# Loading x of tile 1 ahead of Wk and x of tiles 2 to 7 ahead of Wv, with the steps up to the second feed-forward unit in another order and partly on other engines

## The chip, the cores and the metric

The kernel runs on one core of a Trainium2 chip. A core has five engines, each with its own queue of instructions that it works off in order: TensorE (PE in the profile; its weight loads stand apart as PEld), VectorE (DVE), ScalarE (ACT), GpSimd (POOL) and SyncE (SP), which in this kernel issues nearly all DMA transfers. The metric is the device time of one execution in microseconds (us).

## What is computed

A pre-norm transformer block on 2048 rows of width 640: linear attention with 32 heads of width 20, whose feature map is a softmax of a projection and of its negative, and a feed-forward part of width 1728 with SiLU. Inputs and output are bfloat16.

```python
def _A_ref(x, wqkv, w_phi, wo):
    qkv = (x @ wqkv) split into q, k, v and 32 heads
    pq = jnp.einsum("bhsd,hdf->bhsf", q, w_phi)
    pk = jnp.einsum("bhsd,hdf->bhsf", k, w_phi)
    phi_q = jnp.concatenate([_softmax(pq, axis=-1), _softmax(-pq, axis=-1)], axis=-1)
    phi_k = jnp.concatenate([_softmax(pk, axis=-1), _softmax(-pk, axis=-1)], axis=-1)
    kv = jnp.einsum("bhsf,bhsd->bhfd", phi_k, v)
    z  = jnp.einsum("bhsf->bhf", phi_k)
    num = jnp.einsum("bhqf,bhfd->bhqd", phi_q, kv)
    den = jnp.einsum("bhqf,bhf->bhq", phi_q, z)[..., None] + 1e-6
    return heads joined (num / den) @ wo

def _B_ref(x, w1, w2):
    return jnp.einsum("bsf,fd->bsd", _silu(jnp.einsum("bsd,df->bsf", x, w1)), w2)

h  = x + _A_ref(_layernorm(x), A_wqkv, A_w_phi, A_wo)
h2 = h + _B_ref(_layernorm(h), B_w1, B_w2)
```

(The line that splits qkv and the one that joins the heads are shortened to words.)

## The kernel before

The 2048 rows are 16 tiles of 128 rows, t = 0 to 15. Row p * 16 + t of x stands in partition p of tile t, so that one load brings some tiles for all partitions.

The order of all work is written out by hand. ORDER (line 18) is a list of 791 step names; a loop at the end (line 903) calls the step of each name, and a step issues one or a few instructions on its engine. Each engine and each queue then runs its own instructions in the order of the list; waits for data and for free buffers follow from what the steps read and write. A dictionary ON (line 142) says on which engine a step runs where there is a choice, and WARM (line 134) is the number of warm-up matmuls.

The steps, with the lines that issue them (t is a tile, c one of five 128-row chunks of the width, g a half of the output columns):

- X0, X1, X2, X4, X8 (line 161): loads of x, of tiles 0, 1, 2 to 3, 4 to 7 and 8 to 15, 160 KB a tile, on SP's queue. WKc and WVc (line 164): loads of the key and value columns of wqkv, chunk by chunk, 160 KB each. wph0, wph1 (lines 346, 348): the feature weights w_phi in a second layout. load0 to load11 (line 488): wo, w1 and w2 for later.
- warmN (line 215): a 256-column matmul of constants whose result nobody reads.
- The key fold. Projection and feature weights are multiplied ahead, so that one matmul of x gives the keys' features. wkc (line 290) transposes chunk c of Wk on TensorE, wkec (line 307) copies the result out of PSUM, fkc (line 314) multiplies it with phi, which phi_a and phi_b (line 277) build on VectorE, and fkce (line 323) copies that into Wfk.
- The query fold: wqr (line 386) loads a transposed block of wqkv by DMA, phq (line 367) builds phi_q on GpSimd from what own (line 352) made, fqr (line 398) multiplies, fqre (line 404) copies into Wfq.
- Layer norm of tile t: stt (line 432) the moments on VectorE, rst the inverse standard deviation, on GpSimd (lines 441 and 444) or as Ln and Exp on ScalarE (lines 438 and 439), xnt (line 448) the normalized rows on VectorE or GpSimd, xtt the transpose into XnT: for tiles 0 to 3 on TensorE (line 455) with a copy xt on ScalarE or VectorE (line 475, steps x0 to x3), from tile 4 by DMA on SP's queue (line 477).
- Keys and values of tile t: Kt and Vt (line 496) ten 320-column matmuls each; those of tile 0 go chunk by chunk (K0.c line 523, V0.c line 508). ext (line 551) two Exp on ScalarE, sut (line 555) sums on VectorE, rkt (line 563) the inverse of the sums on ScalarE, sct (line 568) a scaling on VectorE, vet (line 572) a copy of the values on ScalarE, kvt (line 587) eleven small matmuls that add the tile to the key-value matrix, in PSUM banks 6 and 7, over all tiles. onesi (line 227) fills constant columns of the buffers of keys and values, mask (lines 245, 239), zeros, eqp and pad other constants, all on GpSimd. bd0, bd1 (line 596) turn the finished key-value matrix into a block-diagonal one.
- Queries: Qt (line 534), qet (line 656), qst (line 660), qrt (line 668 on), qtt (line 684, a transpose by DMA).
- Attention: Dt (line 709), Etg (lines 721, 722: division), ott (line 733: transpose by DMA), Gtg (line 742: output projection), gatg (line 749: residual).
- Second layer norm: lst, lrt, hnt, htt (the last a transpose by DMA, line 769).
- Feed-forward, in units of 2, 4, 4, 4 and 2 tiles that are named by their first tile: uN.f (line 824) and uN.L (line 835), SiLU in sN.f (line 844), ltN (line 856), dtg (line 864), oatg (line 873), outt (line 878).

PSUM has eight banks. Up to the step halves, ps_pair (line 114) hands out banks 0 to 5 as three pairs in turn to wk, xt, fk, fq, K, V and Q steps; a step that takes a pair waits until the reader of what was in it three turns earlier is done. After halves all eight banks go round one by one.

The DMA transfers complete on semaphores that are used in turn, so an issue on SP's queue can also wait for the landing of an earlier transfer.

Of the kernel before, what the change touches and what calls it, by code (L numbers as in the profile page):

```python
# [43 lines left out]
d51 ht8 lr9 hn9 oa21 ga101 G110 out2 ga100 ga110 oa50 oa40 G111 qs14 d41 oa51 D12 ls10 ht7 E120 ht9 u6.1
u6.0 oa41 ga111 u6.12 u6.8 D13 s6.0 s6.1 qr14 s6.8 E121 s6.12 u6.11 ot12 u6.2 u6.3 qr15 lr10 s6.11 u6.L
s6.2 E130 ls11 out4 E131 u6.9 qt15 s6.3 G120 ot13 s6.L u6.6 lt6 s6.6 lr11 u6.7 u6.10 hn10 u6.5 out5 s6.7
hn11 s6.9 u6.4 qt14 G121 ga120 ga121 s6.5 ht11 G130 D14 G131 E140 ga131 s6.10 s6.4 d60 ls12 oa60 d61 d70
ht10 lr12 E141 d91 ga130 ls13 oa61 hn12 oa70 D15 lr13 d90 ht12 ot14 d71 hn13 ht13 out6 G140 oa71 oa90
u10.L oa91 ga140 out9 E150 u10.0 u10.1 out7 E151 u10.6 G141 u10.9 s10.L s10.0 s10.6 u10.8 ga141 d80
u10.7 s10.1 u10.3 u10.11 ot15 s10.3 u10.5 u10.12 oa80 s10.9 s10.8 s10.11 u10.2 u10.4 ls14 s10.7 s10.5  # L50
u10.10 s10.12 s10.4 G150 G151 lt10 lr14 d81 s10.10 s10.2 d110 hn14 oa81 ht14 out8 d111 ga150 d120 ga151
ls15 d101 lr15 d100 hn15 oa100 oa110 ht15 oa101 d121 oa111 out10 oa120 out11 u14.L u14.4 u14.0 oa121
s14.0 s14.L u14.8 u14.6 s14.6 u14.2 d131 u14.12 u14.10 s14.2 s14.4 d130 lt14 oa130 oa131 s14.12 s14.10
# [887 lines left out]
```

## Time and profile before

| | us |
|---|---|
| median of 3 runs (lowest, highest) | 237.5 (237.11, 237.62) |
| the profiled execution | 237.18 |
| its span, first to last instruction | 235.1 |
| TensorE busy | 230.1 |
| VectorE busy | 166.5 |
| ScalarE busy | 104.9 |
| GpSimd busy | 59.9 |
| wk2 / wk3 start | 3.98 / 5.49 |
| K0 starts / its last matmul block ends | 10.34 / 11.70 |
| kv9 starts / kv15 starts / u2.2 starts | 56.83 / 68.59 / 112.56 |

The page gives for each engine the busy time, and in its second part the span in 40 slices of 5.9 us with the busy share in tenths:

```profile
## 2 busy tenths in 40 slices
PE   8999999998999999999999999999999999999995
PEld 5777767776777777877545777645677455778874
DVE  3899998999999999998999896792471330404031
ACT  3998997896869774620234100054300326001410
POOL 5699999990000012211010111011020010100000
```

TensorE is busy from end to end. VectorE is full until about 115 us and then half idle; GpSimd is full from about 10 to 50 us, while it normalizes; ScalarE is fullest in the first 20 us. In the timeline a row has the start, the length, the engine, the line, what is written and read, the number of instructions merged, and in brackets the idle time of the engine before it with what ended it.

Durations of the steps that the change moves: a normalization takes 2.515 us on GpSimd and 0.44 on VectorE (up to 1.00 beside one on GpSimd); the inverse standard deviation 0.80 on GpSimd and 0.50 on ScalarE; a 128x640 copy from PSUM 0.45 on VectorE and 0.70 on ScalarE; Ln and Exp of rk 0.57; the two Exp of one tile's keys 1.30; the sums of a tile's keys 1.43 to 1.48, their scaling 0.82.

### The profile page before, as it was taken

Reading aid. Unit: us, or ns where it says so; the run is one execution under the profiler, and the core shown is the slowest. Engines: PE = TensorE matmul, PEld = TensorE weight load, DVE = VectorE, ACT = ScalarE, POOL = GpSimd, SP = SyncE. Lnnn points to the kernel's source line nnn. Section 1 sums busy time; section 2 is a strip of 40 time slices with the busy share of each in tenths; the row PEclk is TensorE's granted clock in tenths of the full one; section 3 lists DMA queues with packets and bytes.
Section 4 is the critical chain, followed back from the end, with each engine's and each line's share of the span. In section 5 each row is a group of like instructions: output and inputs, shape, how many; then the busy total and the mean of one; then the engine's idle time right before and its main releaser. Section 6 shows DMA issues by size and latency. Waiting matters only on the chain.

```text
span 235.1 us, 5026 instructions
## 1 busy us (share of the span) xinstructions
PE 230.1 (98%) x1984; PEld 160.4 (68%) x1984; DVE 166.5 (71%) x351; ACT 104.9 (45%) x218; POOL 59.9 (25%) x105
## 2 busy tenths in 40 slices
PE   8999999998999999999999999999999999999995
PEld 5777767776777777877545777645677455778874
DVE  3899998999999999998999896792471330404031
ACT  3998997896869774620234100054300326001410
POOL 5699999990000012211010111011020010100000
...
GB/s 175 338 243 91 117 115 170 157 256 246 188 105 74 141 146 93 175 120 91 85 61 128 170 96 173 31 56 172 77 20 91 98 0 28 30 28 56 8 56 56
DMA packets 67213, 26.79 MB, mean 114 GB/s; under 512 B 60151, under 2 KB 66167, under 8 KB 67063
## 3 DMA queue, kind: packets, MB, share of 16 engines
...
q10 hardware_dynamic: 656, 0.03, 0.2%
q14 instruction: 7, 0.06, 0.1%
...
## 4 chain that ended last, share of the span: by engine, by line
PE 72%; DVE 17%; POOL 4%; DMA 2%; issue 2%; SPq 1%; DVEq 0%; POOLq 0%
PE banks L824 22%; PE banks L864 21%; PE banks L742 9%; PE banks L534 8%; PE banks L496 5%; DVE Sk L555 4%; DVE Sq L660 3%; POOL xn L448 3%; DVE st L432 3%; DVE EK L568 2%; PE banks L709 2%; DMA Wv<-in_A_wqkv_dram 2%; PE banks L867 2%; PE banks L587 1%; DVE xn L448 1%
## 5 line engine op out<-in xcount | busy, mean ns | idle before, releaser
L844 ACT ACTIVATE shT<-banks 128x512 bf16<-128x512 f32 (+1 forms) x53 | 28.9, 592 | 83.3 <-PE banks L824 83.3
L864 PE MATMUL banks<-w_sb,shT 128*128 128x320 bf16 (+2 forms) x429 | 61.3, 295 | 0.0
L824 PE MATMUL banks<-HnT,w_sb 128*128 128x512 bf16 (+1 forms) x325 | 59.4, 336 | 0.1
L864 PEld LDWEIGHTS <-shT 128*128 128x128 bf16 x429 | 41.2, 98 | 15.3
L824 PEld LDWEIGHTS <-w_sb 128*128 128x128 bf16 x325 | 31.2, 98 | 22.4 <-issue 0.3
L441 POOL TENSOR_SCALAR rs<-mv 128x1 f32<-128x1 f32 x28 | 8.2, 292 | 141.5 <-DVE mv L433 108.2
L873 DVE TENSOR_TENSOR o_t<-banks,X 128x320 bf16<-128x320 f32 (+2 forms) x33 | 14.8, 474 | 39.6 <-PE banks L867 26.7
L496 PEld LDWEIGHTS <-XnT 128*128 128x128 bf16 x300 | 28.4, 98 | 10.9 <-DMA XnT<-xn 0.3
L432 DVE BATCH_NORM_STATS2 st<-X 128x6 f32<-128x320 bf16 x64 | 27.8, 477 | 3.8 <-DMA X<-in_A_x_dram 3.7
L448 POOL TENSOR_SCALAR xn<-X,mv,rs 128x640 bf16<-128x640 bf16 x10 | 25.1, 2515 | 0.5
L742 PE MATMUL banks<-wo_sb,OT 128*128 128x320 bf16 x160 | 25.1, 299 | 0.0
L656 ACT ACTIVATE EQ<-banks 128x360 bf16<-128x360 f32 (+2 forms) x52 | 22.1, 514 | 5.3 <-PE banks L534 5.1
L660 DVE TENSOR_REDUCE Sq<-EQ 128x66 f32<-128x1320 bf16 x16 | 23.9, 1512 | 0.0
L749 DVE TENSOR_TENSOR X<-banks,X 128x320 bf16<-128x320 f32 x32 | 14.8, 481 | 12.8 <-PE banks L742 12.5
L534 PE MATMUL banks<-Wfq,XnT 128*128 128x360 bf16 (+2 forms) x160 | 23.3, 299 | 0.0
L555 DVE TENSOR_REDUCE Sk<-EK 128x64 f32<-128x1280 bf16 x16 | 23.0, 1460 | 0.0
L551 ACT ACTIVATE EK<-banks 128x640 bf16<-128x640 f32 x32 | 20.8, 707 | 3.7 <-PE banks L587 2.0
L496 PE MATMUL banks<-Wfk,XnT 128*128 128x320 bf16 x150 | 22.5, 299 | 0.0
L496 PE MATMUL banks<-Wv,XnT 128*128 128x320 bf16 x150 | 22.2, 299 | 0.1
L742 PEld LDWEIGHTS <-OT 128*128 128x128 bf16 x160 | 15.1, 98 | 6.3
L534 PEld LDWEIGHTS <-XnT 128*128 128x128 bf16 x160 | 15.1, 97 | 6.1
L444 POOL TENSOR_TENSOR rs<-rs,nhalf_t 128x1 f32<-128x1 f32 x28 | 16.8, 599 | 2.3
...
## 6 DMA issues: line engine op xcount, KB each, us to landing
...
```

Source lines behind the costliest of these rows:

```text
L432: nc.vector.bn_stats(st[:, i, :], X[:, t, i * HD : (i + 1) * HD])
L448: eng.tensor_scalar(out=xn_[t][:], in0=X[:, t, :], scalar1=mv_.pop(t)[:, 0:1], scalar2=rs_.pop(t)[:], op0=ALU.subtract, op1=ALU.mult,)
L496: nc.tensor.matmul(ps[:, g, 0:HD], XnT[:, c, t * P : (t + 1) * P], W[:, c, g * HD : (g + 1) * HD], start=(c == 0), stop=(c == C - 1),)
L534: nc.tensor.matmul(ps[:, 0 : e - a], XnT[:, c, t * P : (t + 1) * P], Wfq[:, c, a:e], start=(c == 0), stop=(c == C - 1),)
L551: nc.scalar.activation(E5[:, :, :, b, :], p4, AF.Exp, scale=sign)
L555: nc.vector.tensor_reduce(sk[t][:], ek[t][:, 0 : H * HF].rearrange("p (q f) -> p q f", f=DH), axis=AX.X, op=ALU.add)
L656: nc.scalar.activation(features(t, a, b)[:, :, :, i], p4, AF.Exp, scale=sign)
L660: nc.vector.tensor_reduce(sq[t][:], EQ[0][:, t, :, 0:FCH].rearrange("p c (q f) -> p c q f", f=DH), axis=AX.X, op=ALU.add)
L742: nc.tensor.matmul(ps[:, 0:HD], ot[t][:, c, :], wo_sb[:, c, g * HD : (g + 1) * HD], start=(c == 0), stop=(c == C - 1),)
L824: nc.tensor.matmul(ps[:, at : at + n], w1_sb[:, c, fc * P : fc * P + P], HnT[u][:, c, 0:n], start=(c == 0), stop=(c == C - 1),)
L844: nc.scalar.activation(shT[u][:, f0 * n : f1 * n], ps_of.pop(("u", u, f0))[:, 0 : (f1 - f0) * n], AF.Silu)
L864: nc.tensor.matmul(ps[:, 0 : b - a], shT[u][:, at : at + P], w2_sb[:, fc, a:b], start=(fc == 0), stop=False,)
```

## The change

Three things change, all in the tables at the head; no function is altered.

1. On SP's queue the load X1 goes from behind WK0 to the place behind X0, ahead of all Wk; X2 and X4 both stand ahead of the Wv loads, where X4 stood between WV0 and WV3 before; wq3 goes ahead of X8, and load6 is the first of the later loads.
2. The steps up to u2.2 stand in another order on all engines. Among others the values of tile 0 come behind the keys of tile 0, V1 ahead of V2, mask and ones at other places, and K, V, Q, D and G steps are interleaved otherwise. From ga61 and u2.2 on the order is as before. Two warm-up matmuls are dropped (20 to 18): 15 ahead of wk2 as before, three behind it instead of five.
3. Some steps run on another engine. xn1, xn2, xn5, xn6 and xn11 go from VectorE to GpSimd, xn3 and xn4 from GpSimd to VectorE; rs3, rs4, rs7, rs8, rs11 and rs12 from GpSimd to ScalarE, rs9, rs13 and rs15 the other way; wke2, x0 and fk3e from ScalarE to VectorE, wke4 from VectorE to ScalarE.

In the diff the lines of ORDER behind u2.2, which are the same words broken into lines otherwise, are left out.

```diff
 ORDER = """
-warm0 warm1 warm2 warm3 warm4 warm5 warm6 warm7 warm8 warm9 warm10 warm11 warm12 warm13 warm14 X0 WK2
-ones0 wk2 warm15 warm16 warm17 warm18 warm19 WK3 wke2 WK0 X1 WK1 st0 wk3 phi_a wke3 wk0 phi_b rs0 xn0
-wke0 own st1 xt0 wk1 fk3 WK4 wke1 X2 wk4 rs1 WV0 wke4 x0 fk1 X4 fk3e WV3 xn1 st2 st3 rs2 WV2 WV4 rs3 fk0
-fk1e fk0e fk4 WV1 V0.0 xn3 xn2 wph1 fk4e fk2 fk2e st6 xt1 wq2 K0s K0.0 K0.4 K0.3 K0.2 K0.1 ones1 x1 st4
-rs4 xt2 K1 ex0 V0.2 st5 x2 ex1 V0.3 rs6 su0 wph0 X8 rs5 K2 xn4 su1 xt4 ex2 wq3 xt3 rk0 sc0 phq V0.1
-ones6 x3 rk1 xn5 ones4 st7 ones5 V0.4 V2 su2 ve2 xt5 ve0 V1 ve1 V3 wq1 xn6 ve3 kv0 sc1 fq2 fq2e st10 K3
-st13 ones2 wq0 V4 ones3 ex3 K4 fq3 rk2 xt6 rs7 ve4 rs13 xn7 V5 ex4 xt7 st8 wq5 su3 fq3e K5 ve5 fq0 st9
-rs10 rk3 wq4 rs8 xn8 kv1 K6 sc2 rs9 kv2 sc3 ex5 xn9 st12 xt8 fq0e ex6 su4 st11 fq1 kv3 xn10 K7 fq1e ex7
-rs11 V6 rk4 su5 fq4 xn13 ve6 xt9 zeros rk5 V8 fq4e V7 sc4 ve8 ve7 xn11 kv4 fq5 st15 V9 rs12 xn12 mask
-load9 fq5e rs15 ve9 K8 xt10 su6 rk6 st14 sc5 su7 K9 kv5 ex8 rk7 su8 Q0 sc6 K10 sc7 xt13 ex9 ones7 kv6
-su9 xn15 rk8 qe0 rs14 ex10 Q1 xn14 kv7 xt11 sc8 load10 xt12 load2 xt15 qe1 K11 su10 load1 load0 V10 V13
-mask0 qs0 kv8 ex11 rk10 ve10 xt14 ve13 rk9 su11 qs1 qr1 V11 K12 sc10 ve11 rk11 K13 sc9 kv9 K14 ex12 kv10
-V12 sc11 ex13 load11 qr0 su12 ex14 load5 kv11 V14 K15 su13 su14 load4 rk12 ve12 rk13 ve14 sc12 sc13 Q2
-rk14 sc14 ex15 kv12 V15 qe2 su15 qs2 mask1 rk15 kv13 kv14 ve15 sc15 Q3 eqp qr2 qe3 kv15 Q5 qe5 Q7 bd1
-load3 halves bd0 qt0 qs3 qr3 qt1 D0 D1 E00 qe7 load6 Q4 Q9 E01 E10 E11 Q6 qe4 Q8 load7 Q10 qe9 qt2 qe6
-ot0 pad0 D2 qs4 qe8 qs5 qr4 G00 E20 ga00 G01 qe10 ot1 Q11 qr5 qt3 E21 D3 G10 ga01 E30 qt4 ls0 G11 E31
-qe11 ga10 lr0 ga11 qt5 Q14 Q12 ot2 Q13 hn0 qe14 ls1 D4 Q15 qs6 lr1 qe12 G20 qe13 qe15 ot3 G21 hn1 E40
-E41 ga20 D5 G30 G31 ga21 ht0 pad1 ht1 u0.L E50 u0.0 ot4 E51 s0.0 ga31 qr6 ga30 ls2 ls3 lr2 u0.4 u0.8 G40
-ga40 s0.8 s0.L load8 qs7 qt6 s0.4 lr3 u0.12 u0.2 hn2 ot5 G41 s0.2 qr7 u0.6 D6 ga41 ls4 u0.10 E60 hn3 lt0
-s0.6 G50 s0.12 G51 s0.10 ga51 ga50 E61 ls5 ht2 lr4 d10 d00 qt7 lr5 ht3 d01 ot6 hn4 hn5 G60 D7 qs8 G61
-qr8 d11 ht5 oa00 ht4 oa10 E70 ga61 u2.2 u2.0 ga60 qt8 E71 ot7 s2.0 oa01 qs9 u2.L qs13 s2.2 qr9 oa11 qs11
...
+warm0 warm1 warm2 warm3 warm4 warm5 warm6 warm7 warm8 warm9 warm10 warm11 warm12 warm13 warm14 X0 ones1
+X1 WK2 wk2 warm15 warm16 warm17 st0 WK3 st1 rs0 wk3 WK0 phi_b WK1 xn0 ones3 wk0 ones7 wk1 xt0 phi_a WK4
+wke2 wke1 wk4 wke3 x0 fk3 wke0 fk1 ones6 wke4 fk3e fk0 fk1e fk0e X2 X4 st2 WV0 WV1 ones5 fk4 fk2 rs1 K0s
+st3 K0.0 WV2 st4 fk4e xn1 fk2e WV3 rs2 K0.1 xt1 K0.3 st5 K0.4 K0.2 V0.0 x1 rs3 WV4 K1 V0.1 ones0 wq2 ex0
+rs4 xn3 ex1 V0.2 xn2 xt2 wph0 x2 wph1 su0 st6 wq3 V1 st7 xn4 V0.3 ve1 su1 rk0 own X8 xt3 x3 K2 ex2 su2
+rs5 phq V0.4 rs6 sc0 V2 st11 ve2 V3 xt4 xn5 st9 rs7 rk1 fq2 K3 st8 ve3 ve0 wq4 V4 fq2e ex3 xn6 rk2 xt5
+ones2 sc1 kv0 K4 ve4 V5 rs8 ex4 fq3 sc2 xn7 su3 st10 rs9 wq0 kv1 ve5 ones4 xt6 su4 K5 fq0 fq3e K6 rk3
+ex5 xt7 kv2 wq1 wq5 fq1 fq0e sc3 ex6 K7 load6 su5 fq1e mask kv3 ex7 xn8 st13 V6 xt8 mask0 rk4 ve6 rk5
+su6 sc4 rs11 fq4 fq4e xn9 zeros st12 V7 ve7 rk6 V8 rs10 sc5 xt9 xn10 load3 V9 su7 ve8 fq5 rs12 rs13 st14
+ve9 xt10 kv4 fq5e rk7 load7 K8 ex8 sc6 kv5 st15 xn11 K9 su8 xn12 sc7 Q0 kv6 K10 xt11 kv7 ex9 Q1 rk8 rs15
+load2 su9 xn13 qe0 ex10 qe1 K11 xt13 sc8 rs14 mask1 rk9 qs0 kv8 xt12 xn14 load11 V10 V13 qr0 ex11 su10
+sc9 xn15 V11 su11 kv9 xt14 rk10 ve13 ve10 K12 load4 ve11 qs1 K13 qr1 xt15 eqp K14 ex12 rk11 sc10 su12
+kv10 ex13 ex14 rk12 V12 load5 V14 sc11 su13 ve12 K15 su14 pad0 sc12 rk13 kv11 qt0 Q2 sc13 ve14 qt1 load0
+rk14 ex15 qe2 kv12 sc14 load1 su15 V15 kv13 rk15 ve15 Q3 qs2 kv14 load9 sc15 kv15 qr2 Q5 Q7 bd1 bd0 qe3
+qe5 halves D0 qs3 Q4 qt2 E00 E01 qe7 qe4 qr3 D1 Q6 E10 Q9 E11 Q8 qe6 qe9 qs4 qr4 qs5 Q10 ot0 qr5 qt3 Q11
+ot1 qe8 qe10 D2 qe11 E20 G00 G01 ga00 E21 D3 E30 qt4 E31 ga01 G10 ga10 ot2 G11 ga11 Q14 Q12 qe14 ot3 ls0
+D4 lr0 G20 Q13 ls1 G30 qe12 lr1 hn0 qt5 E40 G21 G31 hn1 E41 ht0 ht1 ga30 ga20 qs6 Q15 qe13 pad1 ga21 D5
+ga31 qs7 qr6 u0.0 E50 u0.6 qe15 E51 ls3 qr7 ls2 s0.0 load8 u0.L s0.L s0.6 u0.10 ot4 u0.12 u0.8 lr3 G40
+G41 lr2 s0.12 s0.10 u0.4 load10 hn3 qt6 ga41 ot5 ga40 u0.2 s0.8 ls4 D6 lt0 G50 qt7 E60 lr4 G51 E61 ht3
+ga51 s0.2 s0.4 d10 D7 ga50 hn4 ls5 ot6 lr5 hn2 qs8 d00 E70 hn5 oa00 ht2 d01 G60 ht4 G61 qr8 oa10 d11 ht5
+ga61 u2.2 u2.0 ga60 qt8 E71 ot7 s2.0 oa01 qs9 u2.L qs13 s2.2 qr9 oa11 qs11 u2.6 D8 u2.10 E80 ls6 qt9
...
-    WARM = 20
+    WARM = 18
...
 ON = dict(
-        wke2="ACT", wke3="ACT", rs0="POOL", xn0="DVE", wke0="ACT", wke1="DVE", rs1="POOL", wke4="DVE",
-        x0="ACT", fk3e="ACT", xn1="DVE", rs2="POOL", rs3="POOL", fk1e="ACT", fk0e="ACT", xn3="POOL",
-        xn2="DVE", fk4e="ACT", fk2e="ACT", x1="ACT", rs4="POOL", x2="ACT", rs6="ACT", rs5="POOL",
-        xn4="POOL", x3="ACT", xn5="DVE", xn6="DVE", fq2e="ACT", rs7="POOL", rs13="ACT", xn7="POOL",
-        fq3e="ACT", rs10="POOL", rs8="POOL", xn8="POOL", rs9="ACT", xn9="POOL", fq0e="ACT", xn10="POOL",
-        fq1e="ACT", rs11="POOL", xn13="POOL", fq4e="ACT", xn11="DVE", rs12="POOL", xn12="POOL", fq5e="ACT",
-        rs15="ACT", xn15="POOL", rs14="POOL", xn14="POOL",
+        rs0="POOL", xn0="DVE", wke2="DVE", wke1="DVE", wke3="ACT", x0="DVE", wke0="ACT", wke4="ACT",
+        fk3e="DVE", fk1e="ACT", fk0e="ACT", rs1="POOL", fk4e="ACT", xn1="POOL", fk2e="ACT", rs2="POOL",
+        x1="ACT", rs3="ACT", rs4="ACT", xn3="DVE", xn2="POOL", x2="ACT", xn4="DVE", x3="ACT", rs5="POOL",
+        rs6="ACT", xn5="POOL", rs7="ACT", fq2e="ACT", xn6="POOL", rs8="ACT", xn7="POOL", rs9="POOL",
+        fq3e="ACT", fq0e="ACT", fq1e="ACT", xn8="POOL", rs11="ACT", fq4e="ACT", xn9="POOL", rs10="POOL",
+        xn10="POOL", rs12="ACT", rs13="POOL", fq5e="ACT", xn11="POOL", xn12="POOL", rs15="POOL",
+        xn13="POOL", rs14="POOL", xn14="POOL", xn15="POOL",
 )
```

More of the change, by code (lines that the diff above doesn't have):

```diff
@@ L44 @@
[L44 to L53, printed above, removed]
@@ new lines @@
+ga51 s0.2 s0.4 d10 D7 ga50 hn4 ls5 ot6 lr5 hn2 qs8 d00 E70 hn5 oa00 ht2 d01 G60 ht4 G61 qr8 oa10 d11 ht5
+ga61 u2.2 u2.0 ga60 qt8 E71 ot7 s2.0 oa01 qs9 u2.L qs13 s2.2 qr9 oa11 qs11 u2.6 D8 u2.10 E80 ls6 qt9
+u2.7 u2.3 s2.L u2.11 s2.10 s2.6 qr13 E81 u2.9 s2.9 qr11 u2.5 qs12 s2.7 qs10 s2.3 u2.1 D9 G70 s2.5 E90
+qr10 u2.12 s2.11 E91 ot8 G71 u2.4 lr6 ga71 ga70 qt11 out0 lt2 s2.1 qt10 u2.8 out1 hn6 s2.4 qr12 ls7 G80
+s2.8 ga80 ot9 G81 D11 s2.12 E110 d30 ht6 qt13 E111 d20 D10 ga81 lr7 G90 E100 oa30 oa20 E101 ot10 G91 hn7
@@ new lines @@
+ga91 d31 ot11 ga90 ls8 qs15 lr8 d21 qt12 oa31 d50 G100 ls9 G101 hn8 out3 d40 d51 ht8 lr9 hn9 oa21 ga101
+G110 out2 ga100 ga110 oa50 oa40 G111 qs14 d41 oa51 D12 ls10 ht7 E120 ht9 u6.1 u6.0 oa41 ga111 u6.12 u6.8
+D13 s6.0 s6.1 qr14 s6.8 E121 s6.12 u6.11 ot12 u6.2 u6.3 qr15 lr10 s6.11 u6.L s6.2 E130 ls11 out4 E131
+u6.9 qt15 s6.3 G120 ot13 s6.L u6.6 lt6 s6.6 lr11 u6.7 u6.10 hn10 u6.5 out5 s6.7 hn11 s6.9 u6.4 qt14 G121
+ga120 ga121 s6.5 ht11 G130 D14 G131 E140 ga131 s6.10 s6.4 d60 ls12 oa60 d61 d70 ht10 lr12 E141 d91 ga130
```

12 lines of the change are left out of this document (7 added, 5 removed).

## The prediction

> **What bounds the kernel now.** First the page's head and engine table, then the chain of waits, then the list of waits on TensorE, then TensorE's timeline up to 70 us.
>
> ```profile
> span 235.1 us, 5026 instructions
> PE 230.1 (98%) x1984; PEld 160.4 (68%) x1984; DVE 166.5 (71%) x351; ACT 104.9 (45%) x218; POOL 59.9 (25%) x105
> ...
> PE 72%; DVE 17%; POOL 4%; DMA 2%; issue 2%; SPq 1%; DVEq 0%; POOLq 0%
> ...
> PE banks L587 <- DVE EK L568: 0.9, 1, 0.9
> PE banks L215 <- PEq L925: 0.8, 1, 0.8
> PE banks L398 <- DMA WTq<-in_A_wqkv_dram: 0.3, 1, 0.3
> ```
>
> TensorE is busy 98% of the span, and the change removes no matmul but two warm-ups. So it can win only what TensorE waits, and lose only new waits. The listed waits are 0.9 + 0.3 us after the start, but a matmul counts as busy to its modelled end, which hides waits shorter than the drain. The starts show them:
>
> ```profile
> 0.83 3.36 PE L215 MATMUL banks<-const-bfloat16-1.0 128*128 128x256 bf16 x15 [0.83 <-PEq L925]
> 3.98 0.74 PE L290 MATMUL banks<-ident,Wk 128*128 128x128 bf16 x5
> 4.51 1.11 PE L215 MATMUL banks<-const-bfloat16-1.0 128*128 128x256 bf16 x5
> 5.49 0.87 PE L290 MATMUL banks<-ident,Wk 128*128 128x128 bf16 x10
> ...
> 25.08 1.52 PE L496 MATMUL banks<-Wv,XnT 128*128 128x320 bf16 x10
> 26.54 1.52 PE L496 MATMUL banks<-Wfk,XnT 128*128 128x320 bf16 x10
> 28.08 0.44 PE L398 MATMUL banks<-phi_q,WTq 128*128 128x120 bf16 x5
> ...
> 32.44 1.52 PE L496 MATMUL banks<-Wv,XnT 128*128 128x320 bf16 x10
> 34.28 0.44 PE L398 MATMUL banks<-phi_q,WTq 128*128 128x120 bf16 x5 [0.32 <-DMA WTq<-in_A_wqkv_dram]
> 34.86 2.89 PE L496 MATMUL banks<-Wv,XnT 128*128 128x320 bf16 x20
> ...
> 53.09 2.88 PE L496 MATMUL banks<-Wfk,XnT 128*128 128x320 bf16 x20
> 56.83 0.51 PE L587 MATMUL banks<-VP,EK 128*128 128x63 bf16 x11 [0.86 <-DVE EK L568]
> ```
>
> A block of ten 320-column matmuls that is followed at once takes 1.36 us (20.74 to 22.10), five 120-column ones 0.27. So TensorE stands 26.44 to 26.54, 27.90 to 28.08, 33.80 to 34.28, 34.55 to 34.86 and 55.81 to 56.83: 0.10 + 0.18 + 0.48 + 0.31 + 1.02 = 2.1 us. Before kv15 (68.59) the same reading gives 0.2, and from there to the step u2.2 (112.56), where the two orders join again, nothing over 0.05. **2.3 us** is thus all there is to gain behind the opening.
>
> The second engine is VectorE. From 37 to 68.5 us it has no idle time, and kv15 on TensorE starts 0.06 us after sc15 ends (67.71 + 0.82 = 68.53). A gain must come out of VectorE as well.
>
> **The change, part by part.**
>
> **Opening, up to K0.** X1 goes ahead of the five Wk loads, so WK2, which opens the real work, is third on the queue instead of second. Landings before, in order of issue: X0 3.20, WK2 3.88, WK3 5.44, WK0 5.86, X1 6.23, WK1 6.64, WK4 7.28. All five x and Wk loads of 160 KB are equal in size. If a landing goes by its place, wk2 starts at 5.45 instead of 3.98, wk3 at 5.9 instead of 5.49, wk0 at 6.3; from WK1 on both queues have carried the same bytes, so wk1 (6.7) and wk4 (7.3) come as before. If the long step 3.88 to 5.44 belongs to Wk3 itself, WK2 lands near 4.3. I take the places; the other end is no dearer. Dropping two warm-ups (0.21 each at the slow rate) buys nothing, they ran inside this wait.
> The folds: wk4 at 7.3 to 7.7, then wke4 on ScalarE (0.7) to 8.55. VectorE now does st0, st1 (1.1 each), phi_b, xn0, phi_a, wke2, wke1, x0 (0.45 to 0.6 each) to 8.3 and fk3e (bounded by the 0.45 of a bf16 copy and twice the 0.48 of a 320-column fp32 read from PSUM; I take 0.8, nearest the latter) to 9.1. fk4 waits for fk3e's bank pair: 9.1; fk2 9.5 to 9.9. ScalarE then runs fk1e, fk0e, fk4e, fk2e at 0.65 each from 8.6 to 11.2, so K0 ends at 11.75 (before: 11.70). x1 (ScalarE, 0.65) frees K1 at 12.05. By 13.4 TensorE has K1 done, as before at 13.33, but not yet xt2 (0.27): **0.35 us behind**; I take 0.4.
>
> **Wv behind X4.** X4 (640 KB) took 2.6 us of the queue (9.18 to 11.80). Landings become X4 11.0, WV0 11.4, the last Wv near 13.5. V0.0 now comes after K0, near 11.75, V0.1 at 13.4, V1 at 14.3: hidden by 0.3 us or more. Each issue on SP's queue waits for the landing of the one eight before it (X8 was issued at 11.82, X4 landed at 11.80), so X8 now waits for WV1 (11.8) behind wq3 (1.27): 12.9 instead of 11.8, landing near 20.3 instead of 19.5. st11 on VectorE, the first reader, is due at 21.4: hidden by 1 us; if not, VectorE's queue stands.
>
> **Normalization: VectorE to GpSimd.** xn costs 2.515 us on GpSimd (x10, 25.1) and 0.44 on VectorE, up to 1.00 beside a GpSimd xn (36.56). xn1, 2, 5, 6, 11 leave VectorE, xn3 and xn4 go to it: GpSimd has 13 instead of 10 (+7.5 us), and loses rs3, 4, 7, 8, 11, 12 (0.8 each, to ScalarE at 0.5) against rs9, 13, 15: -2.4. Laying the new GpSimd order end to end: xn1 done at 10.0, xn2 13.8, xn5 20.3, xn6 22.8, xn7 25.8, xn8 29.8, xn9 33.0, xn10 36.5, xn11 39.9, xn12 42.4, xn13 45.7, xn14 49.7, xn15 52.3. Adding the 2.5 us from issue to landing of an XnT transpose, the users on TensorE come later: K7 30.7 (28.4 ready), V8 35.7 (34.5, with load6 of 480 KB ahead on the queue), V9 37.0 (35.5), K15 near 60 (55). xt2 starts at 14.0, just when xn2 is there. So hidden, the thinnest cover being 1.2 us at V8.
>
> **VectorE.** From st2 on it loses xn2 .44, xn5 .76, xn6 .35, xn11 .92 and gains xn3, xn4 (0.37 to 1.0 each, I take 0.6): -1.3. It loses the idle 0.50 (X4 landing, 11.83) and 0.78 (rs11, 36.56): -1.3. It starts st2 at 9.1 instead of 8.8: +0.3. New idle: su0 waits for ex0 0.3, sc4 and su8 for ScalarE and K8 together 0.2. Sum -1.8: sc15 ends near **66.7**. TensorE at kv9 then finds sc9 done 1.8 us earlier, and the 1.02 goes.
>
> **ScalarE.** Seven rs instead of four, +1.5 us, against wke2, x0 and fk3e going to VectorE and wke4 coming. Its early queue is dense, as the busy time by stretches shows (columns: all, then PE, PEld, DVE, ACT and POOL, each with its number of instructions, then clock, DMA share, GB/s): ACT 4.87 of 5 us.
>
> ```profile
> 15.00:20.00 5.00, 5.00 (x41) 3.67 (x40) 4.97 (x7) 4.87 (x12) 4.86 (x5) 1.00 0.44 176
> ```
>
> ex3 comes at 23.0 instead of 22.3, ex4 26.0 (25.2), so K5, which needs the banks of K4, waits about 0.2 at 27.2. wq1, now issued behind xt7 (xn7 at 25.8), goes out at 27.1 and lands 3.0 to 4.5 us later as the others did (wq3 20.29 to 23.33, wq1 22.93 to 27.48); fq1 is due at 30.6: 0 to 1.0 wait, I take 0.3. **New waits: +0.5**, bounds 0 and 1.2.
>
> **Attention to u2.2.** The same steps, other neighbours. Walking hn0, hn1 and the transposes after them with the rows above, u0 gets its operands at 91.2 where TensorE arrives at 91.2 (before 92.81), ht5 lands near 109.8 with u2.2 due at 110.9. I price it at 0, with 0.5 either way.
>
> **Sum:** -2.3 + 0.4 + 0.5 = **-1.4 us**; by VectorE -1.8, so TensorE decides. The profiled execution took 237.18 us (span 235.1): 235.8. The median of the runs, 237.5, lies 0.3 above it, and so I put the new one at **236.1**. Best case, no new wait and the opening as before: 237.5 - 2.3 = 235.2; less 0.5 for the attention steps, 234.7.
>
> **A rule against it.** In the rows the clock's opening is seen, not granted (the page grants 1.00 throughout): 256 columns per 0.213 us until 5.2, 0.107 after; five transposes 0.74 at 3.98, 0.44 later. The Trainium skill (TensorE: Matmul & The Clock Gate, Part 1) says the half rate is the default and is lifted by a busy window of some 3.4 us which runs freely; Part 4 adds that transposes do not count as busy in the same way. The trace agrees as far as it goes: it opened after 4.4 us of almost only warm-ups. This is a rival.
>
> Another rule is denied. The Trainium skill (SBUF — State Buffer, SBUF: two separate sides) says that a VectorE operation with two SBUF inputs blocks for the whole of a GpSimd instruction. Here two L568 multiplies took 1.82 us together inside a GpSimd run of three xn (27.51 to 35.02). By the rule three more xn would stall VectorE by up to 7.5 us; I keep the rows.
>
> **Rivals.**
> 1. *The wait moves to ScalarE.* For: 4.6 to 4.9 of 5 us busy from 10 to 20. Against: idle pieces of 0.2 to 0.8 later. If each exp from ex3 to ex7 comes a further 0.3 us late, the pairs of banks hold TensorE by 5 x 0.3 = 1.5: 236.1 + 1.5 = 237.6, no change. Chance 0.13.
> 2. *The clock stays shut.* Place: 3.98 to 5.45, where TensorE now stands for WK2, followed by transposes and three warm-ups. Up to 7.3 it waits for Wk anyway. Before, full rate came 4.4 us after the first matmul (0.83 to 5.2). If the gap does not count at all, it comes at 6.7 (3.15 us before it, 1.25 behind): wk4 starts at 7.7, +0.4. If the count begins anew at wk2, it comes at 9.9: by then 2.2 us of full-rate work is done, through xt0; wk4, five folds of 0.405 and K0 follow, ending at 13.75: +2.0, 238.1. Halfway, at 8.3, it is +1.2: 237.3. It decides for slower from about 9.3 on. Against: 15 warm-ups run unbroken before the gap. Chance 0.18, a third of it no change.
> 3. *GpSimd becomes the bound.* It runs 13 xn in one row; a slip beyond 1.2 us reaches V8, and one more xn's length (2.5) costs 1.3, two cost 3.8: 237.4 to 239.9; slower from a slip of about 3. Against: the ten xn before took 2.50 to 2.53, whatever VectorE did. Chance 0.14, counted as slower.
>
> **How the numbers follow.** Forecast 0.55, the rivals 0.13, 0.18 and 0.14. A measurement here tells about 0.2% (0.5 us) from nothing. Faster 0.55, same 0.13 + 0.06 = 0.19, slower 0.12 + 0.14 = 0.26. The likeliest case's own range is 234.8 to 237.0, from the bounds of the opening, of the new waits and of the attention steps; with rival 1 and all of rival 2 but its end it is 234.8 to 238.2.
>
> **What would show it.** Right: wk2 near 5.4, K0 ending within 0.5 us of 11.75, no wait <-DVE EK at kv9, sc15 ending near 66.7, kv15 near 66.9, u2.2 near 111. Wrong: five transposes of wk0 taking 0.74 (rival 2), a wait of L496 on a DMA XnT at V8 or V9 (rival 3), TensorE gaps ending with ex or ve (rival 1), sc15 later than 68.

## The result, and the profile after

The kernel became slower: 238.54 us median of 25 runs in two comparisons (236.37 to 240.01), where the kernel before took 237.27 (237.03 to 238.34) in the first of them and 237.18 (236.54 to 238.66) in the second. One more run of the changed kernel (242.02) and one of a later kernel were in a slower state, over 1.5% above the fastest of their kernel, and are left out throughout. The two comparisons give a ratio of 1.0051 (95% interval 1.0032 to 1.007) and of 1.003 (1.0002 to 1.0057). Predicted were 236.1, in 234.8 to 238.2. The spread says as much as the median: in the first comparison 16 runs of the kernel before lie within 1.3 us and 15 of the changed one within 2.9; in the second 33 lie within 2.1 and 10 within 3.4. The profiled execution took 237.14 us, the fastest of its 16, so its trace doesn't hold all of the loss.

The page of the changed kernel, its head, its first engine row and the shares of the chain:

```profile
span 235.2 us, 5027 instructions
...
PE 228.5 (97%) x1982; PEld 160.2 (68%) x1982; DVE 166.8 (71%) x350; ACT 104.2 (44%) x222; POOL 65.1 (28%) x102
...
PE 77%; POOL 7%; DMA 6%; DVE 5%; issue 2%; SPq 1%; POOLq 0%; DVEq 0%
```

The list of TensorE's waits in it (total, times, longest):

```profile
PE banks L290 <- DMA Wk<-in_A_wqkv_dram: 1.3, 1, 1.3
...
PE banks L824 <- DMA HnT<-xn: 0.5, 1, 0.5
PE banks L508 <- DMA Wv<-in_A_wqkv_dram: 0.5, 1, 0.5
PE banks L455 <- POOL own_q L352: 0.5, 1, 0.5
```

The last line is xt2: the view names own, the step behind xn2 on GpSimd, but what xt2 reads is xn2, which ended at 15.05, 0.06 us before xt2 starts. The wait at kv9 for VectorE (L587 on EK, 0.9) is gone. In its place stand waits for landings, and GpSimd and the DMA now hold 13% of the chain where they held 6%. TensorE's timeline, with the starts that matter:

```profile
5.49 0.45 PE L290 MATMUL banks<-ident,Wk 128*128 128x128 bf16 x5 [1.30 <-DMA Wk<-in_A_wqkv_dram]
5.78 0.49 PE L215 MATMUL banks<-const-bfloat16-1.0 128*128 128x256 bf16 x3
6.11 1.10 PE L290 MATMUL banks<-ident,Wk 128*128 128x128 bf16 x15
...
12.30 0.43 PE L508 MATMUL banks<-Wv,XnT 128*128 128x320 bf16 x2 [0.51 <-DMA Wv<-in_A_wqkv_dram]
...
31.88 0.44 PE L398 MATMUL banks<-phi_q,WTq 128*128 128x120 bf16 x5
...
49.59 4.24 PE L496 MATMUL banks<-Wv,XnT 128*128 128x320 bf16 x30
...
93.08 2.34 PE L824 MATMUL banks<-HnT,w_sb 128*128 128x256 bf16 x20 [0.54 <-DMA HnT<-xn]
```

Read from start to start, as the prediction did it, the waits won come to 2.1 us, and these are new: 0.68 before V0.0, 0.64 before xt2, 0.27 before fq1, 0.70 before u0.0. So D0 starts at 71.23 (before 71.67), but the first feed-forward unit at 93.08, where before it starts with u0.L at 92.81:

```profile
92.81 0.46 PE L835 MATMUL banks<-w_sb,HnT 128*128 128x64 bf16 x10
```

u2.2 starts at 112.82 (112.56). Even this run, the fastest of its set, has given back by u2.2 all that it won. Behind the start of the unit nothing varies any more: in all thirteen profiles with the changed order and G30 and G31 in their place, 142.1 us pass from u0.0 to the end. What differs between executions lies ahead of it.

### The profile page after: what moved, and what is told of

Read it like the earlier page. It is cut to its first block, busy times and chain, and to the rows that moved or that the text cites. A ratio compares the mean times of both kernels' runs of the same rounds, so it can differ in the third digit from the quotient of the medians.

```text
span 235.2 us, 5027 instructions
## 1 busy us (share of the span) xinstructions
PE 228.5 (97%) x1982; PEld 160.2 (68%) x1982; DVE 166.8 (71%) x350; ACT 104.2 (44%) x222; POOL 65.1 (28%) x102
## 3 DMA queue, kind: packets, MB, share of 16 engines
HBM read 9.64 MB, written 2.62 MB: 52 GB/s over the span
## 4 chain that ended last, share of the span: by engine, by line
PE 77%; POOL 7%; DMA 6%; DVE 5%; issue 2%; SPq 1%; POOLq 0%; DVEq 0%
PE banks L864 24%; PE banks L824 24%; PE banks L496 11%; PE banks L742 7%; PE banks L534 4%; POOL xn L448 4%; DMA X<-in_A_x_dram 3%; PE banks L587 2%; PE banks L867 2%; PE banks L709 2%; DMA HnT<-xn 2%; DMA WTq<-in_A_wqkv_dram 1%; DVE Sq L660 1%; PE banks L835 1%; SPq L164 1%
## 5 line engine op out<-in xcount | busy, mean ns | idle before, releaser
L441 POOL TENSOR_SCALAR rs<-mv 128x1 f32<-128x1 f32 x25 | 6.2, 247 | 136.9 <-DVE mv L433 136.9
L448 POOL TENSOR_SCALAR xn<-X,mv,rs 128x640 bf16<-128x640 bf16 x13 | 34.1, 2629 | 0.3
L722 DVE TENSOR_TENSOR O<-banks,Rd 128x360 bf16<-128x360 f32 (+1 forms) x32 | 15.7, 491 | 1.1
```

The costliest lines, as they stand in the source:

```text
L448: eng.tensor_scalar(out=xn_[t][:], in0=X[:, t, :], scalar1=mv_.pop(t)[:, 0:1], scalar2=rs_.pop(t)[:], op0=ALU.subtract, op1=ALU.mult,)
```

## The experiments

Each kernel was timed beside the kernel before on the same chip; the ratios to it, not the microseconds, are compared across calls. Theory A says that the clock's opening at the start is the loss, B that the order waits on landings with too little cover, C that something late in the kernel is it. In the diffs the lines are shortened around the words that move; WARM goes along with the number of warm-ups, and a step on another engine has its entry in ON changed. All ratios lie within 2% of 1; what is called better or worse rests on their intervals.

**The changed kernel again** (e1, no edit). 

> The changed kernel once more, unaltered, for the profile of an ordinary execution: the one shown (237.14 us) was the fastest of 16 (median 238.7). Theory A (the clock's opening varies): a profile 1 to 2 us longer, in which the five transposes of wk2, wk0 or wk1 take 0.74 us instead of 0.45 and K0 ends after 12.5 us. Theory B (a load that varies): transposes at 0.45, K0 near 11.8, but X2 or Wv lands later than the 10.3 and 12.3 us of the fast profile, with longer waits at V0.0 or xt2. Theory C (something after 20 us varies): the same until xt2 as in the fast profile.

Measured 238.19 (236.37 to 239.79), 1.003 as above. The profile is of the 236.37 run: X2 landed at 8.70 instead of 10.29, V0.0 and xt2 waited for nothing, and fq1 1.13 us:

```profile
29.79 0.50 PE L587 MATMUL banks<-VP,EK 128*128 128x63 bf16 x11
31.27 0.44 PE L398 MATMUL banks<-phi_q,WTq 128*128 128x120 bf16 x5 [0.98 <-DMA WTq<-in_A_wqkv_dram]
```

The same program lands its transfers otherwise from run to run, and the order has no room for it. When X2 is in time the kernel reaches nearly what was predicted, even with fq1 and u0.0 (0.7) waiting.

**Eight more warm-ups ahead of wk2** (e2), so that TensorE doesn't stand there.

```diff
-X1 WK2 wk2 warm15 warm16 warm17 st0 WK3 st1 rs0 wk3 WK0 phi_b WK1 xn0 ones3 wk0 ones7 wk1 xt0 phi_a WK4
+X1 WK2 warm18 warm19 warm20 warm21 warm22 warm23 warm24 warm25 wk2 warm15 warm16 warm17 st0 WK3 st1 rs0 wk3 WK0 phi_b WK1 xn0 ones3 wk0 ones7 wk1 xt0 phi_a WK4
```

> The changed kernel with eight more warm-up matmuls ahead of wk2, so that TensorE has work until about 5.5 us, when WK2 lands. Theory A: the spread of 2 to 5 us goes, the median falls from 238.7 to 237.0 to 237.4, ratio to the kernel before 0.998 to 1.000. Theories B and C: no change, median 238.5 to 239, ratio 1.004 to 1.007.

238.23 (237.69 to 239.54), ratio 1.0045 (1.0027 to 1.0063): no cure. Its profile shows V13 waiting 1.57 us for the transpose of tile 13.

**X1 back behind WK0** (e3).

```diff
-X1 WK2 wk2 warm15 warm16 warm17 st0 WK3 st1 rs0 wk3 WK0 phi_b WK1 xn0 ones3 wk0 ones7 wk1 xt0 phi_a WK4
+WK2 wk2 warm15 warm16 warm17 st0 WK3 WK0 X1 st1 rs0 wk3 phi_b WK1 xn0 ones3 wk0 ones7 wk1 xt0 phi_a WK4
```

> The changed kernel with X1 again behind WK0 on the queue, all else as changed: wk2 starts near 4.0 instead of 5.5 us, the gap on TensorE shrinks from 1.3 to about 0.3 us. Theory A: spread and median fall as with the warm-ups, ratio 0.997 to 1.000. Theory B (X2 and Wv): their place is unchanged, so no change, ratio 1.004 to 1.007.

238.62, 1.0051 (1.0036 to 1.0067). It tells less than it was meant to: st1, which needs X1, stands ahead of xn0 on VectorE, and xt0 waited 1.2 us for xn0.

**The kernel before with seven warm-ups ahead of wk2 instead of fifteen** (e4), so that TensorE stands 1.5 us there.

```diff
-warm0 warm1 warm2 warm3 warm4 warm5 warm6 warm7 warm8 warm9 warm10 warm11 warm12 warm13 warm14 X0 WK2
+warm0 warm1 warm2 warm3 warm4 warm5 warm6 X0 WK2
```

> The kernel before with 7 warm-up matmuls ahead of wk2 instead of 15 (and five behind it as before), so that TensorE stands from 2.3 to 4.0 us, as long as in the changed kernel. Theory A: it is slower than the kernel before by 0.5 to 2 us with a spread as large, ratio 1.003 to 1.008. Theories B and C: no change, ratio 0.999 to 1.001.

238.07, 1.0035 (1.0019 to 1.0051). TensorE runs at half rate (0.74 for five transposes) until 9.8 us, and K0 ends some 1.5 us later. Eight matmuls are gone as well, so this doesn't tell the gap from the smaller amount of early work; one of the two can hold the rate down.

**xn2 on VectorE, ahead of st4** (e5), in the changed kernel.

```diff
-st3 K0.0 WV2 st4 fk4e xn1 fk2e WV3 rs2 K0.1
+st3 K0.0 WV2 fk4e xn1 fk2e WV3 rs2 xn2 st4 K0.1
...
+xn2="DVE"
```

> The changed kernel with xn2 back on VectorE, right behind rs2 and ahead of st4; all else as changed. Theory B (landings on which the new order waits with too little cover): X2 landed at 8.7 to 10.3 us, and rs2 and the 2.5 us of xn2 on GpSimd carry that on to xt2. With xn2 at 0.44 us xt2 no longer waits (0.64 and 0.67 in two of three profiles): own and all later GpSimd work start 2.5 us earlier, so the wait at V13 goes too. Median 237.4 to 238.0, ratio 1.000 to 1.003, smaller spread. Theory A (the clock's opening in the gap): no change, ratio 1.003 to 1.006.

238.02, 1.0019 (1.0001 to 1.0036). xt2 no longer waits; V13 waits 1.69 us.

**xn11 on VectorE and wq1 ahead of xt7** (e6).

```diff
-ex5 xt7 kv2 wq1 wq5 fq1
+ex5 wq1 xt7 kv2 wq5 fq1
...
+xn11="DVE"
```

> The changed kernel with xn11 back on VectorE and wq1 issued ahead of xt7; the opening as changed. Theory B, with the later transposes as the main place: no wait at fq1 (0.27, 1.13, 0.18 and 1.09 us in four profiles) and none at V13 (1.57 in one): median 237.3 to 237.9, ratio 1.000 to 1.003. If the opening is the main place: 238.2 to 238.6, ratio 1.003 to 1.006.

236.69, 0.9982 (0.9961 to 1.0003): the first large step back, so much of the loss lies behind 20 us.

**All of the last two** (e7). 

> Both edits at once (xn2 and xn11 on VectorE, wq1 ahead of xt7). Theory B: every wait on a landing before 60 us goes but that of WK2 and V0.0: median 236.5 to 237.1, below the kernel before, spread about 1 us. Theory A: 238 to 238.5 with the spread of the changed kernel.

237.54 (236.41 to 238.45), 0.9994 (0.9974 to 1.0014). Not better than the pair; its profile opens at half rate, K0 ending 2.0 us late, which led to the runs with warm-ups below.

**X4 behind WV0 again** (e8). 

> The changed kernel with X4 behind WV0 on the queue, as before the change; all else as changed. If the 640 KB of X4 right behind X2 are what makes X2 late: X2 lands near 8.5 us and WV0 near 9.2, V0.0 and xt2 wait no more, against st4 waiting near 12: median 237.5 to 238.0, ratio 1.001 to 1.003. If X2's landing varies by itself: no change, ratio 1.003 to 1.006.

237.57 (236.85 to 239.87), 1.0021 (0.9994 to 1.0049). The wait at V0.0 goes, as it did in e1 without an edit; fq1 (1.19) and u0.0 (1.08) stay. Inconclusive as a cure.

**wq1 ahead of xt7 alone** (e9). 

> One part of the late pair: the changed kernel with wq1 issued ahead of xt7 and nothing else. If the query weights' landing is a main loss (1.13, 1.09 and 1.0 us of waiting at fq1 in three profiles, 0.27 and 0.18 in two), the profile shows no wait of L398 on WTq and the median falls by 0.5 to 0.9 us from the changed kernel's 238.5, to 237.6 to 238.0. If the main loss is the row of normalizations on GpSimd (the late transposes of tile 13), fq1 is cured but the median stays within 0.3 us of 238.5.

238.0 (236.26 to 239.18), 1.0006 (0.9981 to 1.0031). fq1 waits for nothing. The profile of a 238.61 run shows what is left; TensorE at V13:

```profile
48.91 1.52 PE L496 MATMUL banks<-Wv,XnT 128*128 128x320 bf16 x10
52.21 2.89 PE L496 MATMUL banks<-Wv,XnT 128*128 128x320 bf16 x20 [1.79 <-DMA XnT<-xn]
```

V10 and V13 were one run of 30 matmuls in the changed kernel's trace (49.59, 4.24); here V13 starts 1.95 us late. xt13 was issued at 47.76 and landed at 52.17, 4.41 us; in the changed kernel's trace 48.44 to 50.86, 2.42 us, which is 0.09 before V13 starts there. What differs is seen in the DMA view of the stretch that begins at the issue (queue, packets, MB, share; then issues with the median to landing). The changed kernel, 48.4 to 50.7:

```profile
q1 hardware_dynamic: 672, 0.16, 31.6%
issues: line engine op xcount, KB each, median us to landing
XnT<-xn SPq DMA_TRANSPOSE x2, 3.4
```

and this one, 47.8 to 50.1:

```profile
q1 hardware_dynamic: 670, 0.16, 31.6%
q8 instruction: 1, 0.02, 3.8%
issues: line engine op xcount, KB each, median us to landing
XnT<-xn SPq DMA_TRANSPOSE x2, 4.0
```

A packet of instructions (16,384 bytes, here 1.39 us) went through one of the 16 DMA engines while the transpose was under way. The Trainium skill (Runtime: NRT & Kernel Launch, Terms) says that an engine's instruction memory is refilled in blocks of 16 KiB; the packet's size agrees. Of the eight profiles of the changed order that leave xn11 on GpSimd, four have such a packet start 1.2 to 2.0 us after the issue of xt13: it lands 4.0 to 4.4 us after its issue, and V13 waits 1.6 to 2.0. In the other four the packet starts some 0.1 us before the transpose has landed: 2.4 us, and no such wait. The transposes of the second layer norm say the same in all twenty profiles: of the 251 that no such packet met, 96% landed within 2.5 us; of the 65 that met one, 59 took 3.0 to 4.8. The transpose's own packets look alike in the two views (672 and 670); in the four slow cases the landing comes 1.0 to 1.7 us after the instruction packet has ended. Why it comes so late the profile doesn't show.

The two sides of this meeting go by different engines. xt13 goes by GpSimd's row. The packet goes by TensorE: in all profiles with the changed order it starts when 941 to 957 of TensorE's matmuls and weight loads have started, 0 to 1.6 us after V10 starts. So a wait at fq1, which holds TensorE back, moves the packet behind the landing. The three of the eight profiles that wait over 1 us at fq1 (e1, e3, e8) don't wait at V13; of the five others four do. The two losses are not simply added, and curing fq1 alone leaves V13 open to it, as here.

**xn11 on VectorE alone** (e10). 

> The other part: the changed kernel with xn11 on VectorE and nothing else. GpSimd's last four normalizations then end some 2.5 us earlier and xt13 is issued near 46 instead of 48.5. If the slip of GpSimd is a main loss (V13 waited 1.57 us in one profile, 0 in the others), the median falls by 0.5 to 1.2 us, to 237.3 to 238.0, and the slowest runs go most; if wq1 is the loss, it stays within 0.3 us of 238.5, or rises a little by the 0.9 us that VectorE gets to do.

237.85 (236.54 to 238.69), 1.0014 (0.9997 to 1.0032). Each part alone is between the changed kernel and the pair; the two intervals overlap, so they don't tell which part is worth more. This profile opens at half rate; TensorE's timeline:

```profile
5.42 0.71 PE L290 MATMUL banks<-ident,Wk 128*128 128x128 bf16 x5 [1.23 <-DMA Wk<-in_A_wqkv_dram]
5.92 0.85 PE L215 MATMUL banks<-const-bfloat16-1.0 128*128 128x256 bf16 x3
6.56 1.81 PE L290 MATMUL banks<-ident,Wk 128*128 128x128 bf16 x15
```

The same fifteen transposes took 1.10 us in the changed kernel's trace. The work on TensorE is the same up to here as in the changed kernel, and the wait (1.23) is even shorter than there (1.30): the same opening comes to full rate by 5.5 in one execution and near 10 in another.

**The three edits and six more warm-ups ahead of wk2** (e11). 

> The kernel with all three edits (xn2 and xn11 on VectorE, wq1 ahead of xt7; 237.54, from 236.41 to 238.45) with six more warm-ups ahead of wk2, which fill the wait for Wk2 from 4.2 to 5.45. Its profile showed the opening at half rate: 10 to 12 TensorE instructions a microsecond from 6 to 10 us where others have 18 to 20, and K0 ending 2.0 us later. If the clock stays shut in some executions because of the gap, no run is left at the half rate: five transposes take 0.45 throughout, K0 ends near 11.8 in the profile, and the median falls to 236.2 to 236.8 with a spread under 1.5 us. If the spread comes from landings, the median stays at 237.3 to 237.8 and the spread at 2 us.

236.7 (236.28 to 236.79), 0.9958 (0.9942 to 0.9975). The five runs spread over 0.5 us, where the twelve without the warm-ups spread over 2.0. That looks like the clock theory, but twelve runs with the same warm-ups spread over 2.0 again below (e15, e18), so a smaller spread isn't shown. What the opening is worth is seen in the traces of e7 and this kernel, which differ in the warm-ups alone: K0 ends at 13.63 and 11.68, but the spans are 235.8 and 234.8. Of 2.0 us at K0 1.0 is left at the end; V8 and u0.0 wait 0.7 and 0.3 us longer here.

**The same, with G30 and G31 behind D5** (e12).

```diff
-D4 lr0 G20 Q13 ls1 G30 qe12 lr1 hn0 qt5 E40 G21 G31 hn1 E41 ht0 ht1 ga30 ga20 qs6 Q15 qe13 pad1 ga21 D5
-ga31 qs7
+D4 lr0 G20 Q13 ls1 qe12 lr1 hn0 qt5 E40 G21 hn1 E41 ht0 ht1 ga20 qs6 Q15 qe13 pad1 ga21 D5 G30 G31 ga30
+ga31 qs7
```

> The same with the output projections G30 and G31 moved behind D5, so that TensorE has 0.7 us more to do while the transposes of the second layer norm's tile 1 come in. In eight profiles of the changed order u0.0 waited 0.5 to 1.2 us for them. If the wait there is plain lack of work, it falls to 0 to 0.5 and the median falls by 0.5 to 0.7 us under the kernel without the move, to 235.6 to 236.2. If moving the work lets something else come late (ls3 and what follows behind ga31, the landing itself moved), the median stays within 0.2 us.

236.38 (236.22 to 237.11), 0.9959 (0.9943 to 0.9975). TensorE's timeline (the added words shift its lines in the code by one):

```profile
0.83 4.61 PE L216 MATMUL banks<-const-bfloat16-1.0 128*128 128x256 bf16 x21 [0.83 <-PEq L926]
5.51 0.45 PE L291 MATMUL banks<-ident,Wk 128*128 128x128 bf16 x5
...
90.11 1.52 PE L743 MATMUL banks<-wo_sb,OT 128*128 128x320 bf16 x10
91.82 2.34 PE L825 MATMUL banks<-HnT,w_sb 128*128 128x256 bf16 x20 [0.19 <-DMA HnT<-xn]
```

The wait at u0.0 fell from 1.20 us (the kernel without the move) to 0.36 in the starts, as expected, the time by less than was expected of it. kv15 now waits 0.4 us for VectorE (sc15).

**The changed kernel with the six warm-ups alone** (e13). 

> The changed kernel with six more warm-ups ahead of wk2 and nothing else; with the changed kernel (238.5), all three edits (237.5) and all three edits with the warm-ups (236.7) it makes a table of two by two. If the half-rate openings and the late landings add up, the warm-ups are worth here what they are worth there, about 0.8: 237.5 to 237.9, no run under 236.3, and runs over 239 only where V13 or fq1 wait. If the landings hide behind a late opening (what comes 2 us later finds its transposes there), the warm-ups are worth less than 0.4: 238.1 to 238.5.

239.23 (238.4 to 240.48), 1.0076 (1.005 to 1.0101): outside both expectations. The clock opened at 4.1 us, but Wk4 landed at 8.42 (7.12 in the changed kernel's trace), and V13 waited again:

```profile
8.47 0.45 PE L291 MATMUL banks<-ident,Wk 128*128 128x128 bf16 x5 [0.46 <-DMA Wk<-in_A_wqkv_dram]
...
49.41 1.52 PE L497 MATMUL banks<-Wv,XnT 128*128 128x320 bf16 x10
52.55 2.62 PE L497 MATMUL banks<-Wv,XnT 128*128 128x320 bf16 x18 [1.62 <-DMA XnT<-xn]
```

**The kernel before with only the loads' new places** (e14: X1 behind X0, X4 ahead of WV0). 

> The other way round: the kernel before with X1 behind X0 and X4 ahead of WV0 on the queue, and no step moved otherwise. wk2 then waits for the third place, 5.45 instead of 3.98, behind fifteen warm-ups. If the wait in the warm-ups is what makes the clock's opening a matter of luck, the spread of this kernel grows from 1.5 us to 2 or more, with runs near 239 to 239.5, and the median is 237.6 to 238.6. If the loads' places alone are harmless, it stays at 237.2 to 237.7 with the spread of before. V0.0, which stands ahead of K0 here, then waits for WV0 some 2 us and may add up to 1 us by itself.

239.6 (239.48 to 239.72), 1.009 (1.0075 to 1.0105). It opens at half rate:

```profile
5.74 0.71 PE L290 MATMUL banks<-ident,Wk 128*128 128x128 bf16 x5 [1.55 <-DMA Wk<-in_A_wqkv_dram]
...
7.31 1.27 PE L290 MATMUL banks<-ident,Wk 128*128 128x128 bf16 x10
```

**The kernel with G30 and G31 moved, again** (e15). 

> The fastest kernel so far once more, for its interval: 236.2 to 236.9, a ratio near 0.996 to the kernel before.

236.89 (236.43 to 238.42), 0.9983 (0.9965 to 1.0). Over both sets, 19 runs, the median is 236.68.

**The same without added warm-ups and with X1 back behind WK0, st1 behind phi_a** (e16). 

> The three edits and the move of G30 and G31, no added warm-up, and X1 back behind WK0 on the queue, with st1 behind phi_a on VectorE so that xn0 doesn't stand behind it (in the earlier kernel with X1 back it did, 1.2 us). wk2 starts at 3.98 again and TensorE stands nowhere before it. If the gap ahead of wk2 is what costs, this gives what the added warm-ups gave: 236.2 to 236.9 with a spread under 1.5 us. If the earlier X1 itself is worth something, through st1 on VectorE, it is 0.3 to 0.8 slower than the kernel with the warm-ups, again with a small spread. If the clock still opens late (five transposes at 0.74 at 3.98, as in the kernel before, and folds at the half rate beyond 6 us), the runs go up to 238.

237.34 (237.0 to 237.89), 0.999 (0.9978 to 1.0002). The spread is 0.9 us without any added warm-up. But e15, whose gap at wk2 is filled as well, spreads over 2.0 in the same call, so this doesn't show that the gap is what scatters. Wk1 lands at 7.69 and TensorE waits 1.36 us for it, and the kernel stays 0.45 us above the one with early X1 and warm-ups of the same call, with intervals that overlap.

**The loads alone, with six more warm-ups** (e17). 

> The kernel before with X1 and X4 early on the queue (239.6; its profile has five transposes at 0.71 to 0.75 us from 5.7 to 9.6, and K0 ending at 14.0) and six more warm-ups ahead of wk2, nothing else. If the half rate is what the gap costs, TensorE opens at 5.2 as in the kernel before, five transposes take 0.45, K0 ends near 12.2 and the median falls by 1.5 to 2.0 us, to 237.6 to 238.1. If the loads' late landing is the cost, and the rate only goes with it, the median stays at 239.0 to 239.6.

239.11 (238.92 to 240.32), 1.0074 (1.0047 to 1.01). The clock opens at 6.2 and the time falls by 0.5, not by 2: the expectation was wrong. V0.0, ahead of K0 in the old order, waits 1.29 us for a Wv that now comes behind X4; kv9 waits 1.05, about as before. So the late Wv is a cost of its own in the old order, and the change's order, with V0 behind K0, was needed for it.

**The changed kernel with xn11 on VectorE and the six warm-ups** (e18). 

> The changed kernel with xn11 on VectorE and the six more warm-ups (alone 237.85 and 239.23, or 238.19 with eight). If the earlier opening was eaten at V13, whose transpose can't be issued before GpSimd is through its row (48.3 in the profile with the warm-ups, 48.4 in the changed kernel, though TensorE's opening differs), then with the row relieved the warm-ups pay: xt13 is issued near 46, V13 waits for nothing, and the median is 236.9 to 237.5, with fq1 and u0.0 still waiting 1 us each. If the warm-ups themselves cost something, it stays at 237.9 or more.

236.87 (236.2 to 238.3), 0.998 (0.9961 to 0.9999), against 1.0014 and 1.0076 for the two edits alone. TensorE at V10, V13 and V11:

```profile
49.11 4.24 PE L497 MATMUL banks<-Wv,XnT 128*128 128x320 bf16 x30
```

No gap: xt13 was issued at 45.85 and landed at 48.54. This bears out that GpSimd's row eats what an earlier opening wins.

## Why the prediction was wrong

The sum was -2.3 + 0.4 + 0.5 = -1.4; measured were +1.2 and +0.7. Term by term:

**Waits won, 2.3: right to 0.1.** Of the waits that it lists 0.1 of the 0.2 before kv15 is left in the trace after, and kv9 waits for nothing in any trace of the changed order.

**Opening, +0.4: right for some executions, mis-sized for the median.** wk2 was put at 5.45 (5.49), K0's end at 11.75 (11.62). But X4 at 11.0, 2.6 us behind X2, has X2 landing at 8.4, and with X1 early it landed between 8.70 and 10.33. GpSimd's rows show what follows:

```profile
11.53 0.23 POOL L441 TENSOR_SCALAR rs<-mv 128x1 f32<-128x1 f32 x1 [1.69 <-DVE mv L433]
...
12.53 2.52 POOL L448 TENSOR_SCALAR xn<-X,mv,rs 128x640 bf16<-128x640 bf16 x1
...
45.91 2.51 POOL L448 TENSOR_SCALAR xn<-X,mv,rs 128x640 bf16<-128x640 bf16 x1
```

GpSimd stands 1.69 us for the moments of a late X2, xn2 ends at 15.05 instead of 13.8, and TensorE waits at xt2, which the prediction had "just when xn2 is there". WV0, put at 11.4, landed at 12.26, so that V0.0, "hidden by 0.3 us or more", waited 0.68.

**GpSimd's row, "hidden, the thinnest cover being 1.2 us at V8": this step failed.** xn13 was put at 45.7 and ended at 48.42, 2.7 late: 1.25 from xn2, and 1.26 because two normalizations in between, xn6 and xn10, took 3.18 and 3.10 us instead of 2.5. "Whatever VectorE did" held in the kernel before, not here:

```profile
35.86 0.82 DVE L568 TENSOR_TENSOR EK<-EK,Rk 128x1280 bf16<-128x1280 bf16 x1 [0.18 <-ACT Rk L564]
...
35.97 3.10 POOL L448 TENSOR_SCALAR xn<-X,mv,rs 128x640 bf16<-128x640 bf16 x1
```

Both begin while VectorE multiplies two tensors from SBUF, and are longer by nearly the rest of that multiply. Of the 234 GpSimd normalizations of all profiles, the 35 that begin inside such a multiply took 2.62 to 3.18 us; of the 199 others three took over 2.6. In the trace before none begins inside one, so the rows that the prediction kept couldn't show it. It had asked whether VectorE waits for GpSimd, and not whether GpSimd waits for VectorE.

V8 waits 0.55 to 0.67 in three profiles and at most 0.16 in the others. The large wait is at V13; the prediction's list of users leaves it out, though it stands right behind V10 on TensorE, far ahead of V11. And the 2.5 us from issue to landing were taken as fixed, while the same trace of before had one transpose at 2.38 (xt13) and one at 4.10 (ht0). Rival 3 named this mechanism; its place was V13 instead of V8, its price 1.6 to 2.0, paid in four of the eight profiles with xn11 on GpSimd. With xn11 back on VectorE no profile has this wait (e6, e10, e18, and all with the three edits), and with the warm-ups the ratio falls from 1.0076 (e13) to 0.998 (e18), the intervals clear of each other.

**New waits, +0.5: mis-sized.** Their bounds for fq1 were 0 to 1.0, and 0.3 was taken; of nine profiles with wq1 behind xt7, four show 1.09 to 1.19 and five 0 to 0.27. wq1 went out at 28.86 where 27.1 was expected, because xn7, ahead of it by way of xt7, was 1.7 late. ScalarE (rival 1) holds no K step in the traces of the changed order.

**Attention to u2.2, 0 with 0.5 either way: mis-sized.** The operands of u0.0 were put at 91.2 and came at 92.94; the wait is 0.55 to 1.20 us in every profile that leaves G30 and G31 in place. It is the one loss that all of these profiles show, and it is over the bound in each. hn1 is earlier than before (89.09 against 89.78), yet its transpose takes 3.76 us instead of 2.38: ht0 is under way with an instruction packet (88.61), and ht1 is issued only 1.24 us behind ht0, where 2.41 lay between them before.

**VectorE, sc15 near 66.7: followed the rest.** It ended at 68.09 in the changed kernel's trace, where VectorE was not the bound, and at 66.92 in e12 with TensorE's waits mostly gone. There kv15 waits 0.4 us for it, so VectorE bounds once the rest is mended.

**Rival 2, the clock, chance 0.18:** it occurred. Of the eight profiles of the changed order with fifteen warm-ups and X1 early, two open near 10 us, K0 ending at 13.7 (priced: 13.75). With the six or eight more warm-ups, seven of seven had opened by 6.4. It is 2.0 us at K0 and, by e7 and e11, about 1.0 at the end; in a quarter of the executions that would be some 0.25 us of the mean, an estimate from eight profiles. Filling the wait helped where V13 didn't wait (e11, e18) and not where it did (e13, e2).

**The range.** By its own bounds (opening 0 to 0.4, new waits 0 to 1.2, attention 0.5 either way) the likeliest case runs from 234.7 to 237.3, not from 234.8 to 237.0; that doesn't change the outcome.

So the forecast was that of an execution in which nearly everything lands in time; one of 236.37 us was seen, and which execution gets it is luck of the landings. Six profiles of the changed order took 238 us or more: four of them wait at V13 (e2, e5, e9, e13), one has the half rate and fq1 (e10), one fq1 and the wait for xn0 that its own edit brought (e3). What stays open: why Wk4 came 1.3 us late in e13, whether the added warm-ups have a part in it, and how much of the 238.54 each of the waits is in the mean: both traces of the unaltered kernel are of its fastest runs, and a trace shows one execution each.

The kernel with the three edits, the warm-ups and G30 and G31 moved beats the changed kernel, and the one before by 0.2 to 0.4% (0.9959 and 0.9983, the second interval just reaching 1.0).
